# The second layer's output of a token pair by Strassen products of 512-token blocks, in two passes

## The chip, the cores and the metric

One core of a Trainium2 chip runs the whole program. The time is that of the device, in microseconds, from three runs of the kernel before: 595.05 (median), 594.91 and 596.1. A profile of one further execution of the same kernel gives the rows.

## The reference

Retention over q, k, v gives 1536 tokens of 512 features; two gated layers follow, all in float32:

```python
x = attention(q, k, v, lam)            # 1536 x 512
h = np.maximum(x @ moe_w_in, 0)        # 512 -> 2048
x = (h * h) @ moe_w_out                # 2048 -> 512
gate = 1 / (1 + np.exp(-(x @ moe2_w_gate)))   # 512 -> 1536
val = x @ moe2_w_val                   # 512 -> 1536
return (gate * val) @ moe2_w_out       # 1536 -> 512
```

## The kernel before

The tokens form three blocks of 512 (TB). A float32 operand is kept as a high part (a rounded copy, `fp32r`, cast on ScalarE) and a low part (the rest, subtracted on VectorE); a product takes three matmuls: high by high, low by high, high by low. One matmul has 128 x 128 weights and 512 columns of tokens.

Block 0 goes through each layer by itself, unit by unit (a unit is 128 hidden features; 16 in the first layer, 12 in the second): `step_1`, `step_2` (L839, L861). Blocks 1 and 2, the token pair, go through the input side of a layer by Strassen's method: two units and two token blocks make a 2 x 2 problem, seven block products instead of eight, in `strassen` (L646), one call of `block` (L621) for each product, six matmuls in each. The tokens' combinations (T1 to T4) are made by `combine_x` (L554); the weights' (S1 to S4) by `combine_a` (L590), four additions of 128 x 256 on VectorE, after `load_a` (L582) has brought two units from DRAM. `high_a` and `low_a` (L600, L607) split the weights `a` and the sums `as`. In the second layer the keys are (pair i, gate or value), twelve in all; `pair_in_2` (L730) takes the results: gate blocks through the sigmoid, value blocks multiplied by them. The product is a unit's values `g`, 128 features x 512 tokens. `keep_g` (L706) lets the next key store them in DRAM.

After the last key comes the output side of the token pair, `pair_out(2)` (L766): 12 units, each with its values (512 KB) and its output weights (256 KB) loaded by `load_out` and split by `split_out` (L746, L752); per unit 4 column blocks x 2 token blocks x 3 matmuls, into eight banks that stay open from the first to the last unit. At the last unit the banks are copied and stored, the last in two halves on two engines (L798 to L801).

The weights come as float64 and are turned into float32 by `conv_act` and `conv_dve` (two or three operations on ScalarE, three on VectorE) and stored in DRAM as `w32`.

The order of the work is written out by hand. `passed` (L102) counts the matmul time that has been issued (0.2267 us for one, `MM`), and `at(pos, fn)` (L93) puts an operation into its engine's queue when that clock reaches `pos`. T3, T4 and T5 (L881 to L883) are the clock at the start of the second layer's block 0, of the Strassen keys and of the output side. Each engine takes its own queue in order. Tiles come from two pools of 27 buffers (`up`: 128 x 512, `wp`: 128 x 1024), oldest free buffer first; SP issues the loads and stores, and a load waits on SP until its buffer is free. POOL's queue (GpSimd) has no DMAs.

## Time and profile before

| what | us |
|---|---|
| median of the runs | 595.05 |
| the profiled execution | 594.94 |
| its span, first to last instruction | 592.9 |
| TensorE busy | 582.0 |
| VectorE busy | 428.8 |
| ScalarE busy | 349.1 |
| POOL busy | 29.7 |

Engines are PE (TensorE matmul), PEld (its weight load), DVE (VectorE), ACT (ScalarE), POOL (GpSimd) and SP (SyncE, which issues DMAs); a q behind the name is the engine's sequencer. Times are us from the span's start unless marked ns. Matmuls are pipelined: one lasts 389 ns, and the next starts 0.23 us after it.

### The profile page before, as it was taken

The numbers are of one execution on the slowest core, as the hardware profiler recorded it, in microseconds if no ns is written. First come the engines' busy times: TensorE is split into PE (matmuls) and PEld (weight loads), VectorE is DVE, ScalarE is ACT, GpSimd is POOL, SyncE is SP. The second block draws the span as 40 slices with busy tenths as digits, with TensorE's granted clock in tenths as the row PEclk, the third lists the DMA queues.
The fourth block names the chain that finished last, engine by engine and source line by source line (L and its number), as shares of the span: only waits on it lengthen the run. The fifth ranks groups of instructions, "written<-read, shape, count | busy, mean of one in ns | idle before, by whom it ended". The sixth has DMA issues, their size and how long they took to land.

```text
span 592.9 us, 8805 instructions
## 1 busy us (share of the span) xinstructions
PE 582.0 (98%) x3208; PEld 478.7 (81%) x3208; DVE 428.8 (72%) x662; ACT 349.1 (59%) x573; POOL 29.7 (5%) x30
## 2 busy tenths in 40 slices
PE   9899999989999999999999999999999999999997
PEld 8787888767888888888888888888888888888885
DVE  2689896899788868988777787775767786469101
ACT  4679999996655647666457655534455354537101
POOL 1752100000000000000000000000000000000000
PEclk9999999999999999999999999999999999999999
DMA  8999886782163397999968654602233332558003
GB/s 263 413 405 403 286 295 213 256 288 77 71 212 110 111 331 276 414 410 412 405 254 292 250 177 159 179 1 82 96 106 112 137 98 84 193 204 345 0 1 142
DMA packets 52157, 126.94 MB, mean 214 GB/s; under 512 B 5777, under 2 KB 6033, under 8 KB 52114
## 3 DMA queue, kind: packets, MB, share of 16 engines
q1 hardware_dynamic: 51024, 124.15, 58.6%
q10 hardware_dynamic: 1090, 2.24, 1.1%
q8 instruction: 25, 0.41, 0.3%
q14 instruction: 18, 0.15, 0.1%
HBM read 90.71 MB, written 35.66 MB: 213 GB/s over the span
## 4 chain that ended last, share of the span: by engine, by line
PE 88%; DVE 5%; ACT 2%; DMA 2%; issue 2%; POOL 0%; SPq 0%; ACTq 0%; DVEq 0%
PE p L629 32%; PE p L779 26%; PE p L463 15%; PE p L477 10%; PE p L306 2%; PE p L391 2%; DMA decay<-w_dram 1%; DVE at L341 1%; PE p L374 1%; PE p L402 1%; DMA a<-w 1%; DVE m L188 1%; DVE xcl L551 1%; DVE u L180 0%; ACT whi L449 0%
## 5 line engine op out<-in xcount | busy, mean ns | idle before, releaser
L629 PE MATMUL p<-xch,ah 128*128 128x512 f32 x280 | 109.5, 391 | 0.0
L629 PE MATMUL p<-xch,al 128*128 128x512 f32 x280 | 109.0, 389 | 0.0
L629 PE MATMUL p<-xcl,ah 128*128 128x512 f32 x280 | 109.0, 389 | 0.0
L779 PE MATMUL p<-g2h,whi 128*128 128x512 f32 x224 | 87.2, 389 | 0.0
L779 PE MATMUL p<-g2l,whi 128*128 128x512 f32 x224 | 87.1, 389 | 0.0
L779 PE MATMUL p<-g2h,wlo 128*128 128x512 f32 x224 | 87.1, 389 | 0.0
L629 PEld LDWEIGHTS p<-xch,ah 128*128 128x128 f32 x280 | 52.6, 188 | 12.3 <-ACT s L638 1.4
L643 DVE TENSOR_TENSOR c<-p,s 128x512 f32<-128x512 f32 x60 | 41.3, 688 | 28.8 <-PE p L629 22.7
L629 PEld LDWEIGHTS p<-xch,al 128*128 128x128 f32 x280 | 52.6, 188 | 11.1
L629 PEld LDWEIGHTS p<-xcl,ah 128*128 128x128 f32 x280 | 52.6, 188 | 10.6
L638 ACT COPY s<-p 128x512 f32<-128x512 f32 x60 | 35.2, 587 | 37.9 <-PE p L629 37.6
L451 DVE TENSOR_TENSOR wlo<-u,whi 128x512 fp32r<-128x512 f32 x68 | 46.9, 720 | 10.4 <-ACT whi L449 8.4
L155 ACT ACTIVATE j<-raw 128x512 f32<-128x512 f32 x68 | 45.7, 672 | 14.0 <-issue 5.3
L180 DVE CUSTOM_DVE_ANT_0 u<-m,r 128x1024 uint16<-128x1024 uint16 x68 | 48.8, 718 | 5.0 <-ACT r L161 2.0
L779 PEld LDWEIGHTS p<-g2h,whi 128*128 128x128 f32 x224 | 42.1, 188 | 8.8
L779 PEld LDWEIGHTS p<-g2l,whi 128*128 128x128 f32 x224 | 42.1, 188 | 8.7
L779 PEld LDWEIGHTS p<-g2h,wlo 128*128 128x128 f32 x224 | 42.1, 188 | 8.7
L463 PE MATMUL p<-xh,wlo 128*128 128x512 f32 x160 | 43.5, 394 | 3.2 <-DVE wlo L451 3.1
L463 PE MATMUL p<-xh,whi 128*128 128x512 f32 x160 | 43.2, 392 | 0.0
L463 PE MATMUL p<-xl,whi 128*128 128x512 f32 x160 | 42.8, 389 | 0.0
L163 ACT ACTIVATE r<-raw 128x512 int32<-128x512 uint32 x52 | 34.5, 664 | 8.0 <-PE p L779 4.6
L463 PEld LDWEIGHTS p<-xh,wlo 128*128 128x128 f32 x160 | 29.6, 188 | 11.6 <-DVE wlo L451 5.8
(100 smaller groups left out, 922.4 us busy)
## 6 DMA issues: line engine op xcount, KB each, us to landing
raw<-in_w SPq DMA_DIRECT2D x68, 512.0 KB, 6.3
w<-u SPq DMA_DIRECT2D x68, 256.0 KB, 4.7
u<-w SPq DMA_DIRECT2D x64, 256.0 KB, 4.7
g<-g SPq DMA_DIRECT2D x56, 256.0 KB, 4.4
g<-g SPq DMA_DIRECT2D x28, 512.0 KB, 7.5
a<-w SPq DMA_DIRECT2D x20, 512.0 KB, 4.1
kv<-in_kv SPq DMA_DIRECT2D x11, 512.0 KB, 10.3
qk<-in_qk SPq DMA_DIRECT2D x10, 512.0 KB, 9.0
```

The lines of the kernel that those rows point to most:

```text
L155: nc.scalar.activation(j, t[:, :, 1].bitcast(F32), AF.Copy, scale=2.0**-112)
L163: nc.scalar.activation(r, low, AF.Copy, scale=2.0**-29)
L180: nc.vector.tensor_tensor(out=w.bitcast(I32), in0=m, in1=r, op=ALU.add)
L306: nc.tensor.matmul(pv(sc[g])[:, p, :], lhsT=pv(t[:, 1, :])[half(g), p, :], rhs=pv(t[:, 0, :])[half(g), p, :], start=True, stop=True,)
L391: nc.tensor.matmul(o[half(r), p, :], lhsT=v[:, 2 * p + r, :], rhs=pv(at[:, r ^ s, :])[:, p, :], start=p == 0, stop=n == 0 and p == 3, skip ...
L451: lambda lo=lo, src=src, hi=hi: nc.vector.tensor_tensor(out=lo, in0=src, in1=hi, op=ALU.subtract)
L463: nc.tensor.matmul(acc, lhsT=a[:, kk * P : (kk + 1) * P], rhs=b[:, kk, :], start=i == 0, stop=i == 11,)
L477: nc.tensor.matmul(acc[e], lhsT=a[:, e * P : (e + 1) * P], rhs=b, start=first and i == 0, stop=last and i == 2,)
L629: nc.tensor.matmul(acc, lhsT=w[:, col, kk * P : (kk + 1) * P], rhs=x[:, kk, :], start=start and i == 0, stop=stop and i == 5, skip_group_c ...
L638: nc.scalar.copy(s, acc)
L643: nc.vector.tensor_tensor(out=c, in0=acc, in1=s, op=ALU.add)
L779: nc.tensor.matmul(acc[e, t], lhsT=a[:, e * P : (e + 1) * P], rhs=b[:, t, :], start=first and i == 0, stop=last and i == 2,)
```

## The change

The output side of the token pair becomes Strassen products too. The 2 x 2 problem is: two units of a pair by two blocks of 128 output columns, and the two token blocks. There are two passes, one for each half of the 512 output columns. A pass goes through the six pairs; each has seven products of three matmuls of 512 tokens into seven banks, which are combined at the end of the pass. In the second pass pairs 2 and 1 are the last group and go together, and its last product is made in two halves of 256 tokens.

The seven value blocks of a pair are three products of `pair_in_2` as they are and four sums of 512 columns on VectorE (`later`). Pairs 1, 2 and 3 store the seven in DRAM and load them again (`through_dram`; pairs 1 and 2 a second time for the second pass); pairs 0, 4 and 5 are split where they are (`direct`), and the splits of pairs 0, 3, 4 and 5 are kept from the first pass to the second. The seven blocks of the output weights are summed on VectorE in the middle of the second layer (`sum_out_w`) and kept in DRAM; `prepare_w` loads and splits 128 x 896 for each pass and pair.

The sums of the gate and value weights leave VectorE: `load_a` loads the even unit twice into the tile of sums, and `combine_a` issues three DMAs on POOL's queue that add to what is there; the third adds the first's result. The even units' gate and value weights are stored with the other sign; the signs are put right in T1, T2, T4 and in `elem`. `load_a` and `combine_a` of a key stand at the start of the key two before it.

```diff
@@ -171,6 +171,7 @@
+        flip = ph == 2 and u < 2 and f % 2 == 0
...
             lambda: nc.vector.scalar_tensor_tensor(
-                out=m, in0=j, scalar=-(2**31), in1=m, op0=ALU.bitwise_and, op1=ALU.bitwise_or
+                out=m, in0=j, scalar=-(2**31), in1=m, op0=ALU.bitwise_and,
+                op1=ALU.bitwise_xor if flip else ALU.bitwise_or,
...
+        if flip:
+            ops[0] = lambda: nc.vector.tensor_scalar(
+                out=m, in0=j, scalar1=3, scalar2=-(2**31),
+                op0=ALU.logical_shift_left, op1=ALU.bitwise_or,
+            )
...
-            nc.scalar.activation(r, acc[0], AF.Sigmoid)
-            nc.vector.tensor_tensor(out=g, in0=acc[1], in1=r, op=ALU.mult)
+            sign = -1.0 if f % 2 == 0 else 1.0
+            nc.scalar.activation(r, acc[0], AF.Sigmoid, scale=sign)
+            nc.vector.scalar_tensor_tensor(
+                out=g, in0=acc[1], scalar=sign, in1=r, op0=ALU.mult, op1=ALU.mult
+            )
...
+        def minus(name, a, b):
+            t[name] = double("t")
+            nc.vector.scalar_tensor_tensor(
+                out=t[name], in0=t[a], scalar=-1.0, in1=b, op0=ALU.mult, op1=ALU.subtract
+            )
...
+            lambda: diff("T1", b12, b11) if ph == 1 else diff("T1", b11, b12),
...
+            lambda: diff("T2", b22, "T1") if ph == 1 else minus("T2", "T1", b22),
...
+            lambda: diff("T4", b21, "T2") if ph == 1 else minus("T4", "T2", b21),
...
@@ -586,8 +606,28 @@
             out=t.rearrange("p (n h) c -> p n (h c)", n=2),
             in_=w32[ph][2 * i : 2 * i + 2, u].rearrange("n p c -> p n c"),
         )
+        if ph == 2:
+            s = as_t[key] = wp.tile([P, 4, 256], F32, tag="w", name="as")
+            for n in range(2):
+                nc.sync.dma_start(
+                    out=s[:, 2 * n : 2 * n + 2].rearrange("p h c -> p (h c)"),
+                    in_=w32[2][2 * i, u],
+                )
 
     def combine_a(key):
+        ph, i, u = key
+        if ph == 2:
+            s = as_t[key]
+            even, odd = w32[2][2 * i, u], w32[2][2 * i + 1, u]
+            add = dict(accum_op=ALU.add)
+            nc.gpsimd.dma_start(out=s[:, 0:2].rearrange("p h c -> p (h c)"), in_=odd, **add)
+            nc.gpsimd.dma_start(out=s[:, 2], in_=even[:, 256:512], **add)
+            nc.gpsimd.dma_start(
+                out=s[:, 1:4:2], in_=s[:, 0:1].to_broadcast([P, 2, 256]), **add
+            )
+            return
         a = a_t[key]
         s = as_t[key] = wp.tile([P, 4, 256], F32, tag="w", name="as")
...
-        at(pos - 24.0, lambda: load_a(key))
-        at(pos - 15.0, lambda: combine_a(key))
+        at(pos - (24.0 if key[0] == 1 else 42.0), lambda: load_a(key))
+        at(pos - (15.0 if key[0] == 1 else 30.0), lambda: combine_a(key))
...
         part, col = a
+        if key[0] == 2 and part:
+            col = (2, 3, 0, 1)[col]
...
             if n + 2 < len(keys):
                 load_a(keys[n + 2])
+                if key[0] == 2:
+                    combine_a(keys[n + 2])
...
-                combine_a(nxt)
+                if key[0] == 1:
+                    combine_a(nxt)
...
         def use_val(di, t, c, in_psum):
             g = unit("g")
             nc.vector.tensor_tensor(out=g, in0=c, in1=gate.pop((di, t)), op=ALU.mult)
-            keep_g(2, 2 * i + 1 - di, t, g)
+            n = GB.get((di, t))
+            raw[n] = g
+            if n is not None:
+                done(n)
+            if n == 5:
+                later()
+
...
+        def done(n):
+            if i in VIA_DRAM:
+                g = raw[n]
+                at(clock[0] + 2.5, lambda: nc.sync.dma_start(out=gs_dram[i, :, n], in_=g))
+
+        def total(n, a, b, op):
+            raw[n] = unit("gs")
+            nc.vector.tensor_tensor(out=raw[n], in0=raw[a], in1=raw[b], op=op)
+            done(n)
...
+        def later():
+            t = clock[0]
+            at(t + 1.5, lambda: total(0, None, 6, ALU.add))
+            at(t + 3.5, lambda: total(1, 0, 4, ALU.subtract))
+            at(t + 5.5, lambda: total(2, 4, None, ALU.subtract))
+            at(t + 7.5, lambda: total(3, 5, 1, ALU.subtract))
+            at(t + 7.5, lambda: direct(i, raw) if i not in VIA_DRAM else raw.clear())
+    GB = {(0, 0): 4, (1, 0): 5, (1, 1): 6}
+    VIA_DRAM = (1, 2, 3)
+    PIECES = ((0, 1), (2, 3), (4, 5), (6,))
...
+    def new_set(i):
+        both = []
+        for a, b in (("xh", "xr1"), ("xl", "xr2")):
+            if i == 0:
+                s, o = (xp.tile([P, 4, TB], F32R, tag=t, name="gq") for t in (a, b))
+                both.append([s[:, 0:2], s[:, 2:4], o[:, 0:2], o[:, 2:3]])
+            else:
+                p = [double("gq", F32R) for _ in range(3)]
+                both.append(p + [unit("gq1", F32R).rearrange("p (n t) -> p n t", n=1)])
+        gq[i] = both
...
+    def direct(i, raw):
+        pos = clock[0] if i == 0 else DIRECT[i]
...
+        def hi(n):
+            if i not in gq:
+                new_set(i)
+            nc.scalar.copy(block_of(gq[i][0], n), raw[n])
...
+        def lo(n):
+            nc.vector.tensor_tensor(
+                out=block_of(gq[i][1], n), in0=raw.pop(n), in1=block_of(gq[i][0], n),
+                op=ALU.subtract,
+            )
+
+        gap = 2.0 if i == 0 else 0.8
+        for k, n in enumerate((4, 5, 1, 0, 2, 3, 6)):
+            at(pos + gap * k, lambda n=n: hi(n))
+            at(pos + gap * k + 1.2, lambda n=n: lo(n))
...
+    def through_dram(i, load, pos):
...
+        def bring():
+            for p, blocks in enumerate(PIECES):
+                raw[p] = double("gr") if p < 3 else unit("gr1").rearrange("p (n t) -> p n t", n=1)
+            for p in (2, 0, 1, 3):
+                b = PIECES[p]
+                nc.sync.dma_start(out=raw[p], in_=gs_dram[i, :, b[0] : b[-1] + 1])
...
+            nc.scalar.copy(gq[i][0][p], raw[p])
...
+        at(load, bring)
+        for k, p in enumerate((2, 0, 1, 3)):
+            at(pos + 1.1 * k, lambda p=p: hi(p))
+            at(pos + 1.1 * k + 1.3, lambda p=p: lo(p))
+    def sum_out_w(i, pos):
...
+        def load():
+            t["w"] = double("wr")
+            nc.sync.dma_start(
+                out=t["w"], in_=w32[2][2 * i : 2 * i + 2, 2].rearrange("n p c -> p n c")
+            )
...
+        def add():
+            b11, b12, b21, b22 = parts()
+            s = t["s"] = wp.tile([P, 2, 4, P], F32, tag="w", name="ws")
+            for n, a, b in ((0, b12, b11), (1, b22, s[:, :, 0]), (2, b22, b12), (3, b21, s[:, :, 1])):
+                nc.vector.tensor_tensor(out=s[:, :, n], in0=a, in1=b, op=ALU.subtract)
+
+        def store():
+            b11, _, b21, b22 = parts()
+            nc.sync.dma_start(out=wt_dram[i, :, :, 0:4], in_=t.pop("s"))
+            for n, b in ((4, b11), (5, b21), (6, b22)):
+                nc.sync.dma_start(out=wt_dram[i, :, :, n], in_=b)
...
+        at(pos - 9.0, load)
+        at(pos, add)
+        at(pos + 4.0, store)
+    def prepare_w(q, i, load, pos):
...
+        def bring():
+            t["w"] = wp.tile([P, 7, P], F32, tag="w", name="wr")
+            nc.sync.dma_start(out=t["w"], in_=wt_dram[i, :, q])
...
+        def hi():
+            h, _ = wq[q, i] = [wp.tile([P, 7, P], F32R, tag="w", name="wq") for _ in range(2)]
+            nc.scalar.copy(h, t["w"])
...
+        at(load, bring)
+        at(pos, hi)
+        at(pos + 1.2, lo)
+
+
+    PRODUCTS = ((1, 4, 4), (2, 5, 5), (6, 1, 1), (5, 0, 0), (7, 2, 2), (3, 3, 6), (4, 6, 3))
+    STEP = 21 * MM
+    ORDER = (
+        tuple((i,) for i in range(NF2 // 2)),
+        ((5,), (4,), (3,), (0,), (2, 1)),
+    )
+    def blocks_out():
+        for q in range(2):
+            acc, v = {}, {}
...
+            def add(name, k, other, cols=slice(0, TB)):
...
+                nc.vector.tensor_tensor(
+                    out=v[name][:, cols], in0=acc[k][:, cols], in1=v[other][:, cols], op=ALU.add
+                )
...
+            for group in ORDER[q]:
+                first, last = group == ORDER[q][0], group == ORDER[q][-1]
+                for k, gn, wn in PRODUCTS:
+                    if first:
+                        acc[k] = bank()
+                    whole = not (last and q and k == 4)
+                    for cols in (slice(0, TB),) if whole else (slice(0, TB // 2), slice(TB // 2, TB)):
+                        n = 0
+                        for i in group:
+                            (wh, wl), (gh, gl) = wq[q, i], gq[i]
+                            for a, b in ((wh, gh), (wh, gl), (wl, gh)):
+                                nc.tensor.matmul(
+                                    acc[k][:, cols], lhsT=a[:, wn], rhs=block_of(b, gn)[:, cols],
+                                    start=first and n == 0,
+                                    stop=last and n == 3 * len(group) - 1,
+                                    skip_group_check=True,
+                                )
+                                n += 1
+                        if not whole:
+                            add("c21", 4, "u3", cols)
+                            put("c21", 1, 0, cols, nc.sync if cols.start else nc.scalar)
+                    passed(3 * len(group) * MM)
+                    if not last:
+                        continue
+                    if k == 1:
+                        v["s1"] = unit("s1")
+                        nc.scalar.copy(v["s1"], acc[1])
+                    elif k == 2:
+                        add("c11", 2, "s1")
+                        put("c11", 0, 0)
+                    elif k == 6:
+                        add("u2", 6, "s1")
+                    elif k == 5:
+                        add("u4", 5, "u2")
+                    elif k == 7:
+                        add("u3", 7, "u2")
+                        add("c22", 7, "u4")
+                        put("c22", 1, 1, eng=nc.scalar)
+                    elif k == 3:
+                        add("c12", 3, "u4")
+                        put("c12", 0, 1)
+                    elif whole:
+                        add("c21", 4, "u3")
+                        put("c21", 1, 0)
...
@@ -960,7 +1214,7 @@
+        for i in range(NF2 // 2):
+            sum_out_w(i, T3 + 14.0 + 10.0 * i)
...
-        at(T4 - 20.0, lambda: load_a((2, 0, 1)))
-        combine_x([T4 - 46.0 + 3.5 * k for k in range(11)])
+        at(T4 - 32.0, lambda: load_a((2, 0, 1)))
+        at(T4 - 20.0, lambda: combine_a((2, 0, 1)))
+        combine_x(2, [T4 - 46.0 + 3.5 * k for k in range(11)])
...
-        for f in range(NF2):
-            prepare_out(2, f, T5 + 24 * MM * f)
+        for k in range(1, 6):
+            if k in VIA_DRAM:
+                through_dram(k, T5 - 12.0 + 4.0 * k, T5 - 11.0 + 5.2 * k)
+            else:
+                DIRECT[k] = T5 - 11.0 + 5.2 * k
+        for k in range(6):
+            prepare_w(0, k, T5 - 14.0 + STEP * k, T5 - 7.0 + STEP * k)
+        T6 = T5 + 6 * STEP
+        for k, i in enumerate((5, 4, 3, 0, 2, 1)):
+            prepare_w(1, i, T6 - 9.0 + STEP * k, T6 - 3.5 + STEP * k - (2.5 if k == 5 else 0))
+        through_dram(2, T6 + 1.0, T6 + 7.0)
+        through_dram(1, T6 + 6.0, T6 + 12.0)
-        pair_out(2)
+        blocks_out()
```

## Rows read from the trace of the kernel before

**Rows 1.** The page's first part: span; busy us, share and instructions of each engine.
```profile
span 592.9 us, 8805 instructions
PE 582.0 (98%) x3208; PEld 478.7 (81%) x3208; DVE 428.8 (72%) x662; ACT 349.1 (59%) x573; POOL 29.7 (5%) x30
```

**Rows 2.** The chain of waits in order of time: start, length, engine and line, instructions.
```profile
19.60 1.09 PE p L306 x16
...
139.39 2.09 PE p L463 x8
...
523.38 65.31 PE p L779 x288
588.71 0.38 ACT o L800
...
589.11 0.42 DVE o L800
```

**Rows 3.** Busy time by stretches, columns in the first line.
```profile
core 0: us, PE busy (x) PEld busy (x) DVE busy (x) ACT busy (x) POOL busy (x), PEclk, DMA share, GB/s
220.00:310.00 90.00, 90.00 (x398) 74.49 (x397) 76.38 (x115) 56.64 (x87) 0.00 (x0) 1.00 0.93 361
320.00:380.00 60.00, 60.00 (x266) 49.69 (x265) 47.19 (x73) 34.41 (x59) 0.00 (x0) 1.00 0.61 200
444.20:463.20 19.00, 19.00 (x85) 15.73 (x85) 13.61 (x23) 9.27 (x14) 0.00 (x0) 1.00 0.35 111
533.00:543.00 10.00, 10.00 (x46) 8.29 (x45) 9.07 (x10) 7.78 (x11) 0.00 (x0) 1.00 1.04 406
```

**Rows 4.** VectorE's timeline: start, length, instruction, idle before it and its releaser.
```profile
461.97 0.69 DVE L643 TENSOR_TENSOR c<-p,s 128x512 f32<-128x512 f32 x1 [1.36 <-PE p L629]
...
468.89 1.22 DVE L610 TENSOR_TENSOR al<-as,ah 128x1024 fp32r<-128x1024 f32 x1
...
517.49 0.69 DVE L759 TENSOR_TENSOR wlo<-u,whi 128x512 fp32r<-128x512 f32 x1 [4.58 <-ACT whi L755]
...
519.58 0.68 DVE L643 TENSOR_TENSOR c<-p,s 128x512 f32<-128x512 f32 x1
...
523.56 0.68 DVE L759 TENSOR_TENSOR wlo<-u,whi 128x512 fp32r<-128x512 f32 x1
524.16 1.22 DVE L760 TENSOR_TENSOR g2l<-g,g2h 128x1024 fp32r<-128x1024 f32 x1
525.30 0.68 DVE L739 TENSOR_TENSOR g<-p,r 128x512 f32<-128x512 f32 x1
...
584.63 0.69 DVE L792 COPY o<-p 128x512 f32<-128x512 f32 x1 [33.41 <-PE p L779]
```

**Rows 5.** The same of SP's and ScalarE's queues around key 6's cast of sums.
```profile
448.10 0.37 SPq L585 DMA_DIRECT2D a<-w  x1
...
467.59 1.06 ACT L604 CAST ah<-as 128x1024 fp32r<-128x1024 f32 x1 [1.03 <-DVE as L598]
468.70 0.59 ACT L638 COPY s<-p 128x512 f32<-128x512 f32 x1
```

**Rows 6.** DMA: packets and issues (KB, us to landing), 525 to 545; then 406, 586, whole.
```profile
DMA packets 2568, 6.91 MB, mean 346 GB/s; under 512 B 287, under 2 KB 287, under 8 KB 2568
g<-g SPq DMA_DIRECT2D x9, 512.0 KB, 7.8
...
g<-g SPq DMA_DIRECT2D x23, 256.0 KB, 4.3
...
out_t<-o SPq DMA_DIRECT2D x3, 256.0 KB, 2.1
...
kv<-in_kv SPq DMA_DIRECT2D x11, 512.0 KB, 10.3
```

**Rows 7.** VectorE's groups by line and form: busy us, mean ns, idle before.
```profile
L451 DVE TENSOR_TENSOR wlo<-u,whi 128x512 fp32r<-128x512 f32 x33 | 21.0, 686 | 7.3 <-ACT whi L449 5.4 <-DMA u<-w 0.8 <-issue 0.7
...
L188 DVE SCALAR_TENSOR_TENSOR m<-j,m 128x512 int32<-128x512 int32 x11 | 7.6, 693 | 0.4
...
L185 DVE TENSOR_SCALAR m<-j 128x512 int32<-128x512 int32 x11 | 4.6, 420 | 0.0
...
L596 DVE TENSOR_TENSOR as<-a 128x256 f32<-128x256 f32 x11 | 4.6, 418 | 0.0
```

More of the change, by code (lines that the diff above doesn't have):

```diff
@@ L192, in conv_dve @@
         ]
+        if flip:
[3 more added lines that the diff above has]
+            )
         if sign:
+            assert not flip
             ops.pop(1)
@@ L552, in split_x, with combine_x @@
         )
-    def combine_x(places):
+    def combine_x(ph, places):
         x1, x2 = xr[1], xr[2]
@@ new lines, in block_of @@
+    def block_of(pieces, n):
+        return pieces[n // 2][:, n % 2]
+    def direct(i, raw):
+        pos = clock[0] if i == 0 else DIRECT[i]
+        raw = dict(raw)
+        def hi(n):
[11 more added lines that the diff above has]
+            at(pos + gap * k + 1.2, lambda n=n: lo(n))
@@ new lines, in retention_moe_kernel, with hi, lo @@
+    DIRECT = {}
+    def through_dram(i, load, pos):
+        raw = {}
+        def bring():
[4 more added lines that the diff above has]
+                nc.sync.dma_start(out=raw[p], in_=gs_dram[i, :, b[0] : b[-1] + 1])
+        def hi(p):
+            if i not in gq:
+                new_set(i)
+            nc.scalar.copy(gq[i][0][p], raw[p])
+        def lo(p):
+            nc.vector.tensor_tensor(
+                out=gq[i][1][p], in0=raw.pop(p), in1=gq[i][0][p], op=ALU.subtract
+            )
[3 more added lines that the diff above has]
+            at(pos + 1.1 * k + 1.3, lambda p=p: lo(p))
@@ new lines, in prepare_w, with lo @@
+    def prepare_w(q, i, load, pos):
+        t = {}
+        def bring():
[4 more added lines that the diff above has]
+            nc.scalar.copy(h, t["w"])
+        def lo():
+            h, l = wq[q, i]
+            nc.vector.tensor_tensor(out=l, in0=t.pop("w"), in1=h, op=ALU.subtract)
+        at(load, bring)
+        at(pos, hi)
+        at(pos + 1.2, lo)
@@ new lines, in retention_moe_kernel, with put @@
+    PRODUCTS = ((1, 4, 4), (2, 5, 5), (6, 1, 1), (5, 0, 0), (7, 2, 2), (3, 3, 6), (4, 6, 3))
[7 more added lines that the diff above has]
+            acc, v = {}, {}
+            def put(name, t, e, cols=slice(0, TB), eng=nc.sync):
+                col = (t + 1) * TB
+                eng.dma_start(
+                    out=out[2 * q + e, :, col + cols.start : col + cols.stop],
+                    in_=v[name][:, cols],
+                )
+            def add(name, k, other, cols=slice(0, TB)):
+                if name not in v:
+                    v[name] = unit(name)
+                nc.vector.tensor_tensor(
+                    out=v[name][:, cols], in0=acc[k][:, cols], in1=v[other][:, cols], op=ALU.add
+                )
+            for group in ORDER[q]:
[14 more added lines that the diff above has]
+                                    skip_group_check=True,
+                                )
+                                n += 1
[25 more added lines that the diff above has]
+                        put("c21", 1, 0)
+                for i in group:
+                    wq.pop((q, i))
+                    if q or i < 3 and i:
+                        gq.pop(i)
@@ L785, in pair_out @@
                     copy = nc.scalar.copy if t == 0 else nc.vector.tensor_copy
-                    if ph == 1:
-                        copy(xr[t + 1][:, e, :], acc[e, t])
-                        continue
-                    dst = out[e, :, (t + 1) * TB : (t + 2) * TB]
-                    if (e, t) != (3, 1):
-                        o = unit("o")
-                        copy(o, acc[e, t])
-                        (nc.scalar if t == 0 and e < 3 else nc.sync).dma_start(out=dst, in_=o)
-                        continue
-                    for c, copy, eng in (
-                        (0, nc.scalar.copy, nc.scalar),
-                        (TB // 2, nc.vector.tensor_copy, nc.sync),
-                    ):
-                        o = unit("o")[:, 0 : TB // 2]
-                        copy(o, acc[e, t][:, c : c + TB // 2])
-                        eng.dma_start(out=dst[:, c : c + TB // 2], in_=o)
+                    copy(xr[t + 1][:, e, :], acc[e, t])
     prev = []
```

21 lines of the change are left out of this document (13 added, 8 removed).

## The prediction

> **What bounds the kernel now.** I read the page's busy shares first: TensorE is busy 98% of the span, VectorE 72%, ScalarE 59% [rows 1]. A busy TensorE need not be at its pace, so the chain of waits came next. From 139.39 us to 588.71 us it is 32 pieces, all TensorE; what waits there are lies in the attention part ahead of them, and the output stage that the change replaces is one unbroken piece of 288 matmuls in 65.31 us, 0.2268 us each [rows 2]. So before 588.71 us a matmul less is 0.2268 us less, as long as operands, banks and queues keep up. The table by stretches shows what is in reserve: the granted clock is 1.00 and TensorE full in each; VectorE is busy 13.6 of 19 us while one pair of units is made, 9.1 of 10 us just after the output stage begins [rows 3], and has nothing to do for the 33.4 us before its next to last copies [rows 4]. Behind the last matmul come a half copy on ScalarE, one on VectorE that waited for it, and a store, till 592.9 [rows 1, 2].
>
> I write S for 523.4 us, where the output stage begins; on the code's own clock it is T5. A key is one of the twelve Strassen products before S: 42 matmuls, 9.52 us; key 6 begins near 464.7.
>
> **The change part by part.**
>
> *Matmuls.* 12 units x 24 = 288 become 2 column halves x 6 pairs x 7 products x 3 = 252. 36 x 0.2268 = 8.2 us less. The last six matmuls are each cut into two of 256 columns. No row has that form. Below, half of 0.2268 each costs nothing; above, a full 0.2268 each costs 6 x 0.2268 = 1.4 us. Sixteen matmuls of 128 columns take 1.09 us, 0.068 each [rows 2], so the weight load does not hold a short matmul at the long one's pace: I take 0.1 us.
>
> *The tail.* Before: ScalarE's half copy, 0.38, then VectorE's, 0.42, then the store [rows 2]. Now VectorE's addition of the last half reads the bank with no copy of ScalarE's ahead: 0.4 us less.
>
> *VectorE in the first half of the new stage.* This is where the gain can go. Seven blocks of values are split for a pair where four were, twice for pairs 1 and 2, and twelve times 896 columns of weights where 512 were. From the starts of VectorE's own instructions when they queue: 0.60 us for 512 columns (523.56 to 524.16), 1.14 for 1024 (524.16 to 525.30) [rows 4]; 896 lie between, 1.0. The first low half of pair 1 can start near S-4.9: ScalarE's cast for it stands behind the copy of S1 x T1 in the last key, which TensorE ends at S-6.8; copy 0.59 and cast 1.06 [rows 5] follow. Up to the low half of weights 3, VectorE then has in order: pairs 1 and 2, 3 x 1.14 + 0.6 each, 8.0; three of four pieces of pair 3, 3.4; weights 1, 2 and 3, 3.0; the last key's seven additions and products at 0.6, 4.2, which before too began at S-3.8 [rows 4]; the four sums of the last pair, 2.4. Together 21.0: it ends at S+16.1. TensorE wants it after three pairs of 21 matmuls, at S+14.3: a wait of 1.8, with semaphores 2.0. The same sum for weights 2 (14.2 us, done at S+9.3, wanted at S+9.5) and for the first value of the last pair (S+22.5, wanted at S+23.8) gives none. Bounds: 0 if casts come earlier than their places; with unqueued durations, 0.69 and 1.22, the list is 23.7 long and the wait 4.5; with loads 1.5 us late besides, 6. I take 2.0. In the second half the list is some 17 us in 28.6: nothing.
>
> *Loads of that stage.* Before, 512 KB landed in 7.8 us while the engines moved 346 GB/s, since all came after S [rows 6]. The new ones start as buffers of the last keys come free, from about S-18: 5.5 MB of values for pairs 1 to 3 and 2.8 MB of weights by S+14, 8.3 MB in 32 us, 260 GB/s: nothing on the path, and if they lag, it is in the 6 above.
>
> *Sums of the gate and value weights by DMA.* VectorE loses 8 additions a pair at 0.42 [rows 7] and gains 4 sums of 512 columns at 0.69: 2.8 for 3.4, and pair 0's seven splits, 4.8 us over two keys, fit the 5.4 of 19 that are idle [rows 3]. The added wait is ScalarE's: its cast of the sums waits for three DMAs on POOL's queue, the third of which waits for the other two. Behind the cast stands ScalarE's copy of S1 x T1, and for that TensorE's fourth block of the key: in key 6 the copy ends at 469.29 [rows 5], the block begins at 464.7 + 5.44 = 470.1, 0.8 us of slack. The time there is: the load that feeds the cast at 467.59 was issued at 448.10 [rows 5], since SP runs ahead until a buffer of an older key is free. The two new loads are issued about 1 us behind it. With 4.3 us to land [rows 6] and X for each of two adding DMAs in a row, the sums are ready 1 + 4.3 + 2X after 448.10, and must be by 20.3 (19.5 and the slack): X up to 7.5. Keys 7, 9 and 11 have less: ahead of their load stand now, in SP's order, stores of split values up to the pair's second sum, which VectorE reaches some 7 us into the key; the load moves from 2.5 to 7.2 us into it, and X may be 5.2. No row has an adding DMA, nor any on POOL's queue. Bounds for 256 KB: 2.1 (an output store) and 10.3 (the slowest row, of 512 KB, as if what is read and added counted double) [rows 6]. I take 4.3, the row of the same size in the same stage: no wait, 1.8 us to spare in the tight keys.
>
> The Trainium skill's "DMA: Bandwidth & Descriptors", section "Anatomy of one DMA — SWDGE (gpsimd) path", gives 2.0 us plus bytes over 436 GB/s for a DMA of POOL's queue, an estimate of 2.6 us for 256 KB, with nothing said of adding; by it the sum stays and the spare time is 5.2 us. The nearest row says 4.3.
>
> *Sums of the output weights, between 325 and 385 us.* 24 additions of 256 columns at 0.42 [rows 7], 10 us, on a VectorE that is busy 47.2 of 60 us there [rows 3]. What is left, 2.7 us, is their cover; without it the splits of the next unit come late. Their 8.3 MB in 60 us come to 200 GB/s that move there now; the stage before moved 361 [rows 3]. Between 0 and 2 us; I take 0.2.
>
> *The signs.* Second operations in instructions that are there already: a three-operand form takes 693 ns where the plain split takes 686 [rows 7]. Nothing; if the shift went from 420 ns to 690, 12 x 0.27 = 3.2 us, spread over conversions that are not due.
>
> *Sum.* 594.94 (the profiled execution: span 592.9 and 2.0 around it) - 8.2 + 0.1 - 0.4 + 2.0 + 0.2 = 588.6; the median of the runs shown, 595.05, is 0.1 higher: 588.8 rounded up.
>
> **The rivals.**
> *1. VectorE's list decides the stage.* For: 21 us in a row, where 9.1 of 10 were full before [rows 3]. Against: before, it stood idle 4.6 us just ahead [rows 4]. With the long durations and pair 1 late by 2 us and more, and a wait between 325 and 385 us, 5 to 8 us are lost: 592 to 595.5, most of the gain.
> *2. The adding DMAs take too long (the slower side).* Place: ScalarE's cast of the sums, keys 2 to 11. It costs from X = 5.2 and decides from 6.5: three tight keys x 2 x 1.3 = 7.8, 596.5. For: three DMAs in a row, each reading what it writes. Against: nothing else is on POOL's queue. At X = 8.3 all keys are 1.6 late over two keys, 0.8 a key for nine, 7, and the tight ones 4 more each: 588.8 + 19 = 608; at 10.3 it is 2.7 a key and 4 more thrice: 625.
> *3. POOL's issue waits for VectorE.* VectorE runs 8.1 us of a key without a gap, thirteen instructions from 461.97 on [rows 4]. An issue held till such a run ends waits 8.1 x 8.1 / (2 x 9.52) = 3.4 us on average; two in the chain make X 7.7 in effect: 0.1 a key and 5 in each tight one, 16 us: 605. Against: in that stage VectorE's rows are TENSOR_TENSOR at 0.69 for 512 columns, none at the shift's 0.42 [rows 4, 7]. The Trainium skill's "SBUF — State Buffer", section "Who interferes with whom", says that VectorE's two-port forms, copies and one-operand arithmetic, keep POOL from the memory altogether, and that two-operand additions do not take the port that writes; by that rule the rows speak against this rival.
> *4. All is hidden:* 594.94 - 8.2 + 0.1 - 0.4 = 586.4, if the casts run 2 us ahead of where I put them.
>
> **How the numbers follow.** Forecast 588.8, chance 0.60, its own range 587.2 to 592. Rival 1: 0.17 (0.10 faster, 0.07 no change). Rival 2: 0.13 (slower). Rival 3: 0.04 (0.03 slower, 0.01 no change). Rival 4: 0.06. Within 0.2%, 1.2 us, can't be told from no change here. So faster 0.60 + 0.10 + 0.06 = 0.76, the same 0.08, slower 0.16. The range goes from 586.3 (rival 4 within) to 598 (rival 1 and the mild end of rival 2 within); about 0.13 is left out above.
>
> **What would show it.** Right: 252 matmuls' worth in the last stage, S to its end about 59 us; one TensorE wait near S+14 for a low half on a VectorE that is unbroken from S-5 to S+27; ScalarE's cast of the sums some 3 us into the key as before; adding DMAs near 4.3 us. Wrong: waits of TensorE inside the keys for ScalarE's copy behind a cast that waits for POOL's DMA; waits between 325 and 385 us; 5 us or more of waits after S; or waits for a bank where the column halves meet.

## The result and the profile after

The changed kernel takes 597.94 us (median of 10 runs, 596.57 to 601.98), the kernel before 594.9 in the same comparison: a ratio of 1.0058, with an interval of 1.0038 to 1.0078. It is slower, by 0.6%; 588.8 us was forecast. Its runs spread with TensorE's granted clock: the four with a mean of 0.998 or more take 596.6 to 597.5 us, the six below it 597.5 to 602.0. The profiled execution, one of the six, took 598.35 us; its span is 3.7 longer than before. The page's first part, as [rows 1]:

```profile
span 596.6 us, 9061 instructions
PE 578.2 (97%) x3178; PEld 472.4 (79%) x3178; DVE 464.2 (78%) x702; ACT 366.9 (62%) x599; POOL 65.6 (11%) x66
```

TensorE is busy 3.8 us less, in a longer span. What it waited for (total us, times, longest), without the rows of the attention part and of the units' weights:

```profile
PE p L671 <- ACT s L680: 4.7, 3, 2.1
...
PE p L975 <- DVE wq L930: 1.3, 2, 0.8
...
PE p L671 <- DVE c L685: 0.6, 1, 0.6
...
PE p L975 <- DVE c L960: 0.5, 1, 0.5
```

L671 is the matmul of the Strassen keys, L975 that of the new output stage. The first row is the sign that the prediction had named for its slower rival: TensorE waits inside the keys for ScalarE's copy. The chain of waits (start, length, what), as [rows 2]:

```profile
310.77 10.88 PE p L471 x48
...
457.20 6.59 DMA as<-w
464.31 0.86 POOL as L626
465.16 3.80 issue
468.98 3.81 DMA as<-as
...
473.89 0.59 ACT s L680
474.52 4.54 PE p L671 x12
...
497.44 26.25 PE p L671 x114
...
532.72 8.88 PE p L975 x39
...
592.32 0.99 PE p L975 x6
```

Before, this chain is TensorE alone from 139.39 us on [rows 2]. Now a load, two adding DMAs and a copy (457.20 to 474.48) are a part of it. Its pieces say where the time went; the kernels of the last four columns are told below:

| us in the profiled execution | before | after | value stores later | sums on VectorE | adding DMAs alone | sums on VectorE, weight sums later |
|---|---|---|---|---|---|---|
| up to T3 | 310.9 | 310.8 | 311.4 | 310.7 | 311.1 | 311.3 |
| block 0, T3 to T4 | 95.2 | 96.8 | 96.8 | 96.8 | 95.2 | 96.7 |
| keys, T4 to S | 117.3 | 125.2 | 121.4 | 120.2 | 118.3 | 120.2 |
| output stage | 65.3 | 60.6 | 60.5 | 60.2 | 65.3 | 60.1 |
| behind the last matmul | 4.2 | 3.3 | 3.3 | 3.2 | 4.1 | 3.2 |
| span | 592.9 | 596.6 | 593.3 | 591.1 | 594.0 | 591.4 |

The output stage gave 4.7 us and the tail 0.9. The keys took 7.9, block 0 another 1.6. The queues around the longest wait, as [rows 5]: SP's, POOL's, ScalarE's and TensorE's timelines (start, length, instruction, idle before it and its releaser):

```profile
453.46 2.66 SPq L797 DMA_DIRECT2D gs<-gs  x2
456.22 0.39 SPq L605 DMA_DIRECT2D a<-w  x1
456.69 0.93 SPq L612 DMA_DIRECT2D as<-w  x2
...
462.22 0.91 POOL L625 DMA_DIRECT2D as<-w  x1 [9.08 <-ACT ah L644]
464.31 0.86 POOL L626 DMA_DIRECT2D as<-w  x1 [1.17 <-DMA as<-w]
468.98 1.21 POOL L627 DMA_DIRECT2D as<-as  x1 [3.82 <-DMA as<-w]
...
472.94 1.04 ACT L644 CAST ah<-as 128x1024 fp32r<-128x1024 f32 x1 [3.97 <-DMA as<-as]
473.89 1.07 ACT L680 COPY s<-p 128x512 f32<-128x512 f32 x2
...
474.52 0.50 PE L671 MATMUL p<-xch,ah 128*128 128x512 f32 x1 [2.09 <-ACT s L680]
474.86 0.40 PE L671 MATMUL p<-xcl,ah 128*128 128x512 f32 x1
```

Read downwards: stores of values, of which three more stand before these two, hold SP's queue from 448.15 on, and the three loads come behind them; the first adding DMA goes out 6.0 us after the first load, the second 2.1 us later, since it waits for the other load; the one that adds the first's result goes out at 468.98 and lands 3.8 us later; ScalarE, idle for 3.97 us, runs the cast and then the copy that TensorE waits for. The same idle time on the same releaser comes twice more, 3.86 us before 495.86 and 1.66 before 515.00: the casts for keys 7, 9 and 11 and no others.

Busy time by stretches, as [rows 3]; the third stretch is the twelve matmuls after that wait:

```profile
core 0: us, PE busy (x) PEld busy (x) DVE busy (x) ACT busy (x) POOL busy (x), PEclk, DMA share, GB/s
320.00:380.00 60.00, 59.04 (x260) 48.19 (x259) 50.24 (x88) 30.13 (x52) 2.90 (x3) 1.00 0.99 330
444.20:463.20 19.00, 19.00 (x86) 15.61 (x85) 16.49 (x24) 11.12 (x19) 3.92 (x4) 1.00 0.86 235
474.50:479.10 4.60, 4.58 (x13) 3.61 (x14) 2.04 (x4) 1.09 (x2) 1.21 (x1) 0.63 0.92 209
```

The DMA engines, 0.35 busy over a pair of keys before, are 0.86 busy, and 0.99 instead of 0.61 at 320 to 380. The granted clock, 1.00 in every stretch of [rows 3], is 0.63 behind the wait of 2.09 us: most of the twelve matmuls start 0.43 us apart instead of 0.23, which is the lower of the clock's two levels (1.2 GHz). They take 4.54 us where twelve take 2.72.

DMA issues of the keys (KB each, median us to landing), as [rows 6]:

```profile
as<-w SPq DMA_DIRECT2D x18, 256.0 KB, 5.7
...
as<-w POOLq DMA_DIRECT2D x9, 256.0 KB, 4.5
as<-as POOLq DMA_DIRECT2D x9, 256.0 KB, 4.9
...
as<-w POOLq DMA_DIRECT2D x9, 128.0 KB, 5.6
```

VectorE's timeline, as [rows 4], at one place of block 0 and one of the output stage:

```profile
339.33 0.42 DVE L904 TENSOR_TENSOR ws<-wr,ws 128x256 f32<-128x256 f32 x1
...
341.46 1.88 DVE L459 TENSOR_TENSOR wlo<-u,whi 128x512 fp32r<-128x512 f32 x3
...
547.15 1.08 DVE L930 TENSOR_TENSOR wq<-wr,wq 128x896 fp32r<-128x896 f32 x1
```

From 338.20 to 341.46 four output-weight sums (the last is copied) and a conversion's three operations stand ahead of the low half `wlo` of a unit's weights; TensorE waits 0.60 us for it at 342.20, and 0.36 in the same way at 351.02. At 547.15 VectorE reaches the low half of weights 3 after a list without a gap; it ends at S+15.5, and TensorE has waited 0.81 us.

### The profile page after: what moved, and what is told of

Read it like the earlier page. It is cut to its first block, busy times and chain, and to the rows that moved or that the text cites. A ratio compares the mean times of both kernels' runs of the same rounds, so it can differ in the third digit from the quotient of the medians.

```text
span 596.6 us, 9061 instructions
## 1 busy us (share of the span) xinstructions
PE 578.2 (97%) x3178; PEld 472.4 (79%) x3178; DVE 464.2 (78%) x702; ACT 366.9 (62%) x599; POOL 65.6 (11%) x66
## 4 chain that ended last, share of the span: by engine, by line
PE 74%; DVE 9%; DMA 7%; issue 5%; ACT 5%; POOL 1%; ACTq 0%; SPq 0%; DVEq 0%; POOLq 0%
PE p L671 24%; PE p L1048 15%; PE p L471 14%; PE p L485 9%; PE p L975 7%; PE p L314 2%; PE p L399 2%; DMA as<-as 1%; DMA wr<-wt 1%; DMA decay<-w_dram 1%; DMA as<-w 1%; DVE at L349 1%; DVE m L189 1%; PE p L382 1%; PE p L410 1%
## 5 line engine op out<-in xcount | busy, mean ns | idle before, releaser
L671 PE MATMUL p<-xch,ah 128*128 128x512 f32 x280 | 110.5, 394 | 5.3 <-ACT s L680 4.7
L671 PE MATMUL p<-xch,al 128*128 128x512 f32 x280 | 109.7, 392 | 0.0
L671 PE MATMUL p<-xcl,ah 128*128 128x512 f32 x280 | 109.6, 392 | 0.0
L671 PEld LDWEIGHTS p<-xch,ah 128*128 128x128 f32 x280 | 53.0, 189 | 19.3 <-ACT s L680 7.3
L671 PEld LDWEIGHTS p<-xch,al 128*128 128x128 f32 x280 | 52.9, 189 | 11.1
L671 PEld LDWEIGHTS p<-xcl,ah 128*128 128x128 f32 x280 | 53.0, 189 | 10.8
L975 PE MATMUL p<-gq,wq 128*128 128x512 f32 (+1 forms) x258 | 58.9, 387 | 1.8 <-DVE wq L930 1.3
L975 PEld LDWEIGHTS p<-gq,wq 128*128 128x128 f32 x258 | 47.4, 188 | 13.4 <-DVE wq L930 3.0
L625 POOL DMA_DIRECT2D as<-w x12 | 12.1, 1007 | 347.1 <-PE p L471 287.8
L1048 PE MATMUL p<-g2l,whi 128*128 128x512 f32 x128 | 49.8, 389 | 0.0
L1048 PE MATMUL p<-g2h,wlo 128*128 128x512 f32 x128 | 49.8, 389 | 0.0
L1048 PE MATMUL p<-g2h,whi 128*128 128x512 f32 x128 | 49.8, 389 | 0.0
L457 ACT CAST whi<-u 128x512 fp32r<-128x512 f32 x68 | 38.0, 614 | 1.5 <-PE p L485 1.0
```

The costliest lines, as they stand in the source:

```text
L457: nc.scalar.copy(hi, src)
L625: nc.gpsimd.dma_start(out=s[:, 0:2].rearrange("p h c -> p (h c)"), in_=odd, **add)
L671: nc.tensor.matmul(acc, lhsT=w[:, col, kk * P : (kk + 1) * P], rhs=x[:, kk, :], start=start and i == 0, stop=stop and i == 5, skip_group_c ...
L975: nc.tensor.matmul(acc[k][:, cols], lhsT=a[:, wn], rhs=block_of(b, gn)[:, cols], start=first and n == 0, stop=last and n == 3 * len(group) ...
L1048: nc.tensor.matmul(acc[e, t], lhsT=a[:, e * P : (e + 1) * P], rhs=b[:, t, :], start=first and i == 0, stop=last and i == 2,)
```

## The experiments

### The adding DMAs, the output side, or both

Four kernels make a square. In one the output side stays as changed and the sums are VectorE's again:

```diff
-            nc.gpsimd.dma_start(out=s[:, 0:2].rearrange("p h c -> p (h c)"), in_=odd, **add)
...
+            tt(out=s[:, 0], in0=a11, in1=a21, op=ALU.add)
+            tt(out=s[:, 2], in0=a21, in1=a22, op=ALU.add)
+            tt(out=s[:, 3], in0=a22, in1=s[:, 0], op=ALU.add)
+            tt(out=s[:, 1], in0=a12, in1=s[:, 3], op=ALU.add)
```

> The changed kernel with the sums of the gate and value weights as four additions of 256 columns on VectorE again, no adding DMA and no second load of the even unit. Theory A and theory B both expect the waits for the cast of sums to go: the keys take 117.3 to 119 us, 591 to 593 us in all. A third theory C (VectorE is the bound of the keys once it has the value sums too, and the DMAs only took the place of that) expects TensorE to wait for VectorE or for copies behind it by 4 us or more in the keys: 596 or more.

593.47 us, ratio 0.9973 [0.9961, 0.9985]: faster than before, 0.5 above the range that A and B expect, and far from C. The waits behind the adding DMAs are gone, but the keys still take 120.2 us: TensorE waits 0.62 and 0.96 us for ScalarE's copy among the casts of pair 0 (443.48 and 454.25; ahead of the second, ScalarE stands 1.73 us for VectorE's key sums) and 0.60 at the end.

The other has the adding DMAs and the signs with the output side of before, and what prepares it:

```diff
-        blocks_out()
+        pair_out(2)
```

> The kernel before with the signs, the double load and the adding DMAs alone; the output side, its stores and its splits as before. Theory A: with the stores of values held to the next key as before, the load of a key keeps about two keys' time, the cast of sums waits nowhere, and the time is that of before within 0.5 us (594.5 to 595.5). Theory B: TensorE waits in most keys, 598 or more.

595.82 us, ratio 1.0012 [1.0001, 1.0023]: 0.3 above theory A's range, far from B's. In its keys TensorE waited once:

```profile
PE p L670 <- ACT s L679: 0.8, 1, 0.8
```

and in this stretch the DMA share is no lower than in the changed kernel:

```profile
440.00:460.00 20.00, 20.00 (x90) 16.56 (x89) 11.32 (x15) 10.07 (x16) 6.01 (x6) 1.00 0.94 231
```

| median us | sums on VectorE | adding DMAs |
|---|---|---|
| output side as before | 595.0 | 595.8 |
| Strassen output side | 593.5 | 597.9 |

The adding DMAs alone cost 0.8 us (0.1 to 1.4 by the interval), the output side alone gains 1.5. Independent, both together would give 594.3; the 3.6 us above that, some 1.5 either way by the three intervals together, come of their meeting. With the adding DMAs alone a key's loads go out on SP every 9.5 us (the next at 459.08 and 468.60), and the chain of DMAs fits:

```profile
440.04 0.37 SPq L604 DMA_DIRECT2D a<-w  x1
...
449.56 0.37 SPq L604 DMA_DIRECT2D a<-w  x1
```

In the changed kernel they go out at 440.24, 456.22, 460.19 and 476.29: every second one is late. The DMAs themselves are no faster alone; the issues of its keys (406 to 524), where the changed kernel has 5.7 and 4.9 us:

```profile
as<-w SPq DMA_DIRECT2D x18, 256.0 KB, 5.4
...
as<-as POOLq DMA_DIRECT2D x9, 256.0 KB, 6.3
```

### SP's order

```diff
-                at(clock[0] + 2.5, lambda: nc.sync.dma_start(out=gs_dram[i, :, n], in_=g))
+                at(clock[0] + 12.0, lambda: nc.sync.dma_start(out=gs_dram[i, :, n], in_=g))
```

> The changed kernel with the stores of the split pairs' values put 12.0 us on the clock behind the value instead of 2.5, so that in SP's order the next key's load stands ahead of them; nothing else. Theory A (those stores hold the loads of keys 7, 9 and 11 back, and the three adding DMAs then miss the cast): the three waits of TensorE in the Strassen keys (2.1, 2.0 and 0.2 us) and the slow clock after the first (1.8 us) go, the keys take 118.5 us instead of 124.9, about 592 us in all. Theory B (the adding DMAs are too slow by themselves under this load, whenever they begin): waits of 1 to 2 us stay in at least two keys, 596 us or more.

593.87 us, ratio 0.9974 [0.996, 0.9988], nearer to theory A. The stores now stand behind the next loads, and 3.8 of the 7.9 us in the keys are back. TensorE's waits at the two places:

```profile
474.39 0.50 PE L671 MATMUL p<-xch,ah 128*128 128x512 f32 x1 [1.38 <-ACT s L680]
484.76 0.50 PE L671 MATMUL p<-xch,ah 128*128 128x512 f32 x1 [0.53 <-ACT s L680]
```

2.09 and 1.98 us became 1.38 and 0.53, and the clock is 1.00 in the stretches behind both. So the order of SP's queue makes half of the keys' loss. Not all: the load of key 7's sums goes out at 453.50, 3.8 us earlier in its key (this run's keys begin 0.6 us later), but its cast starts at 472.81, only 0.7 us earlier, because the last adding DMA, issued at 465.21, needs 7.4 us; the stores run beside the adding DMAs now, with a DMA share of 1.05 to 1.15 from 474 to 489. How much of the rest is this traffic, and how much POOL's own order (a key's last DMA ahead of the next key's first), no run parts.

The three loads on ScalarE's queue were the second try:

```diff
-        nc.sync.dma_start(
+        (nc.scalar if ph == 2 else nc.sync).dma_start(
...
-                nc.sync.dma_start(
+                nc.scalar.dma_start(
```

> The changed kernel with the second layer's three loads of a key (both rows, and the first row twice) issued by ScalarE instead of SyncE; adding DMAs, stores and everything else unchanged. Theory A, it is SyncE's order (value stores ahead of the loads) that makes keys 7, 9 and 11 late: their loads go out at the key's start, the waits of 4.7 us and the slow clock after the longest go, 592.5 to 594 us. Theory B, the chain of load, adding DMA, adding DMA is long by itself with 16 DMA engines 0.85 to 0.95 busy: more than half of the waits stays, 595.5 us or more.

608.78 us, ratio 1.0227 [1.0198, 1.0255]. By the number it is theory B, but the run doesn't test it: ScalarE reaches the loads in its own order, at 418.20, 424.20, 438.57, 444.65 and 460.01, every second one late again, and eight waits of 11.3 us in all follow.

### Block 0: the output-weight sums

```diff
-                nc.vector.tensor_tensor(out=s[:, :, n], in0=a, in1=b, op=ALU.subtract)
+                nc.gpsimd.tensor_tensor(out=s[:, :, n], in0=a, in1=b, op=ALU.subtract)
```

> The changed kernel with the 24 subtractions for the output weights issued on POOL instead of VectorE. If VectorE's list is what makes TensorE wait between 340 and 351 us, the 1.6 us that block 0 of the second layer takes longer than before go (95.2 us from 310.8 on instead of 96.8), 596 us in all. If the added DMA traffic is (the engines' share is 0.98 at 320 to 340 us), the 1.6 us stay.

600.21 us, ratio 1.0087 [1.0059, 1.0115], not the 596 expected; block 0 takes 97.0 us. The waits for `wlo` are gone, two for ScalarE's `gh` (0.28 and 0.64 us) came. While GpSimd subtracts (343.2 to 346.9) VectorE's operations of 0.69 us take 1.1:

```profile
343.32 1.14 DVE L189 SCALAR_TENSOR_TENSOR m<-j,m 128x512 int32<-128x512 int32 x1
344.50 1.11 DVE L181 CUSTOM_DVE_ANT_0 u<-m,r 128x1024 uint16<-128x1024 uint16 x1
```

The next run moves the sums behind the conversions:

```diff
-            sum_out_w(i, T3 + 14.0 + 10.0 * i)
+            sum_out_w(i, T3 + 48.0 + 8.0 * i)
```

> The changed kernel, with the six output-weight sums (loads, four subtractions each, stores) moved from 325 to 375 us to 359 to 399 us (one every 8 us), behind the last conversions of weights. Theory A, the four subtractions ahead of a low half of weights on a VectorE that is 90% busy at 340 to 360 cost block 0 its 1.6 us: the waits at 342.20 and 351.02 go, the block takes 95.2 to 95.5 us instead of 96.8, about 596.3 us. Theory B, the traffic does it (DMA share 0.9 to 1.0 at 340 to 360, 0.6 before): with the loads and stores at 350 to 404 beside the keys' own first loads, as much is lost there, 597.5 us or more.

605.04 us, ratio 1.0173 [1.0133, 1.0213]; neither theory had this. The waits at 342.20 and 351.02 are gone, as theory A says, but one of 1.55 us for a cast came at 401.19, and the last sums' stores are now ahead of key 2's load on SP (411.35; 387.31 in the changed kernel):

```profile
409.15 2.15 SPq L910 DMA_DIRECT2D wt<-wr  x3
411.35 0.61 SPq L605 DMA_DIRECT2D a<-w  x1
```

```profile
431.44 0.80 PE L671 MATMUL p<-xch,ah 128*128 128x512 f32 x1 [5.49 <-ACT s L680]
```

Behind these 5.49 us the granted clock is 0.56 from 431.4 to 436. It is a late load and the adding chain once more, by another store.

### The rest of the loss, without adding DMAs

First the low halves of the output weights on GpSimd, in the changed kernel:

```diff
-            nc.vector.tensor_tensor(out=l, in0=t.pop("w"), in1=h, op=ALU.subtract)
+            nc.gpsimd.tensor_tensor(out=l, in0=t.pop("w"), in1=h, op=ALU.subtract)
```

> The changed kernel, with the low halves of the output weights (12 subtractions of 128x896, the tile whose lateness held TensorE 0.81 us at 548.28 and 0.46 us at 582.77) computed by GpSimd instead of VectorE. Theory A, VectorE's unbroken list from 528 to 564 is what makes these halves late: both waits go, the output stage shortens by 1.3 us or a little more, about 596.5 us against 597.9 of the changed kernel. Theory B, GpSimd is the worse place: its subtractions of 128x256 took 0.73 to 1.19 us where the weight sums were put on it, which is 2.6 to 4.1 us for 128x896, and VectorE's copies of 0.69 us took 1.1 us beside them; then the waits stay or change their name, 598 us or more. Keys and block 0 stay as in the changed kernel in both.

603.87 us, ratio 1.017 [1.0119, 1.0222]: theory B. The output stage takes 65.6 us, all that it had gained. VectorE's third sum of values is 0.68 us in the changed kernel (540.33); here it and the operation behind it take 2.61 us each while GpSimd's two run:

```profile
541.01 2.61 DVE L801 TENSOR_TENSOR gs<-gs,g 128x512 f32<-128x512 f32 x1
543.54 2.61 DVE L876 TENSOR_TENSOR gq<-gr,gq 128x512 fp32r<-128x512 f32 x1
...
540.16 5.44 POOL L930 TENSOR_TENSOR wq<-wr,wq 128x896 fp32r<-128x896 f32 x2 [4.84 <-ACT gq L873]
```

Additions with one operand in a PSUM bank (`c<-p,s`) stay at 0.68. The Trainium skill's "SBUF — State Buffer", section "Who interferes with whom", says that a VectorE instruction with two inputs in SBUF contends with a GpSimd instruction that reads SBUF, and that one with at most one such input, outside its two-port modes, does not. The trace agrees, 2.61 against 0.68 us.

Then all three: sums on VectorE, weight sums later (48 + 8i), low halves on GpSimd; and the same with `gap` 3.4 for pair 0 instead of 2.0:

> The three repairs together: the keys' sums on VectorE again with no adding DMA, the output-weight sums behind the conversions, and the low halves of the output weights on GpSimd. If each is worth what its own run says: 593.5 of the first alone, less 1.6 (weight sums later), less 1.3 (low halves): 590.6 us, and 592 if GpSimd's subtraction gives nothing. Rival: with 24 subtractions more at 359 to 399 and the keys' four additions, VectorE is over 85% busy from 360 to 520 and gives a part back as waits in the keys: 592.5 us or more.

> As the three repairs together, and the seven casts of pair 0's blocks 3.4 us apart instead of 2.0. In the kernel with the sums on VectorE, TensorE waited for ScalarE's copy 0.62 us at 443.48 and 0.96 us at 454.25, both among these casts. Theory A, the casts' crowding makes these waits: they go, 1.0 to 1.6 us below the run of the three repairs (about 589.3 us). Theory B, they only move along with the casts, or the four-block additions on VectorE make them: within 0.4 us of that run.

598.34 us, ratio 1.0051 [1.0034, 1.0068], and 600.27, 1.0079 [1.0053, 1.0104]. The first is far above its 590.6: an output stage of 65.8 us, spoilt in the same way, not the waits in the keys that its rival expected. Block 0 takes 95.8 us, so the place of the sums was worth 1.0 there. In the second the waits of 0.62 and 0.92 us among pair 0's casts (442.73, 453.48) became 1.15 and 0.79 at 461.03 and 463.47: by the traces, which both span 596.4 us, they move along, theory B. Its median is 1.9 us above the first's all the same: its four runs have a mean granted clock of 0.996 or 0.997, the first's 0.999 or 1.00.

With the low halves on VectorE, and the weight sums at 46 + 7i:

```diff
-            sum_out_w(i, T3 + 14.0 + 10.0 * i)
+            sum_out_w(i, T3 + 46.0 + 7.0 * i)
```

> The keys' sums on VectorE again (no adding DMA, no second load), and the six output-weight sums from T3+46 on, one every 7 us, behind the conversions; the low halves stay on VectorE. Theory A, the two losses are independent: 593.5 us of the sums on VectorE alone, less the 1.0 us that block 0 came out shorter with the sums later (95.8 us from T3 to T4 against 96.8): 592.5 us, with the output stage as in that run (0.83 us at its first wait for a low half). Theory B, the later sums push VectorE's preparation of the keys back: 593.5 us or more, with new waits between 390 and 460.

593.45 us, ratio 0.997 [0.9959, 0.9981], where 593.47 had been measured without the move: theory B. The two waits in block 0 went and one of their size came, for a cast:

```profile
396.64 1.22 DVE L582 SCALAR_TENSOR_TENSOR t<-t,xr 128x1024 f32<-128x1024 f32 x1
...
397.89 1.05 ACT L560 CAST xch<-t 128x1024 fp32r<-128x1024 f32 x1 [3.76 <-DVE t L582]
...
399.51 1.20 PE L471 MATMUL p<-xh,whi 128*128 128x512 f32 x4 [0.97 <-ACT whi L457]
```

The cast `whi` stands on ScalarE behind the cast of a token combination (`t`), which VectorE ends only at 397.86: four weight sums (388.78 to 390.3) and four key sums (395.17 to 396.7) are in its list ahead. The same loss, at another crowded place.

```diff
-            prepare_w(0, k, T5 - 14.0 + STEP * k, T5 - 7.0 + STEP * k)
+            prepare_w(0, k, T5 - 18.0 + STEP * k, T5 - 11.0 + STEP * k)
...
-            prepare_w(1, i, T6 - 9.0 + STEP * k, T6 - 3.5 + STEP * k - (2.5 if k == 5 else 0))
+            prepare_w(1, i, T6 - 14.0 + STEP * k, T6 - 5.0 + STEP * k - (2.5 if k == 5 else 0))
```

> As the run with both repairs, and the output weights prepared earlier: the first six loads, casts and low halves 4 us earlier, the loads of the last six 5 us earlier and their casts 1.5 us. Theory A, the waits for low halves near 15.7 us and 49.8 us into the output stage come from VectorE's unbroken list (first) and from a load that lands after 8.7 us (second): both go, 1.3 us below the run with both repairs, or a little more. Theory B, VectorE has no room before the output stage either (9.4 of 10 us busy at 520 to 530): the earlier low halves delay the last copies of the keys, the wait at the stage's start (0.60 us) grows, and less than 0.4 us is won.

593.42 us, ratio 0.9976 [0.9966, 0.9987]: no gain, theory B. The first wait for a low half (0.81) went, the one at the stage's start grew from 0.60 to 0.88 us and the second from 0.32 to 1.37.

```diff
-                eng.dma_start(
+                (eng if q else nc.scalar).dma_start(
...
-            sum_out_w(i, T3 + 46.0 + 7.0 * i)
+            sum_out_w(i, T3 + 46.0 + 6.0 * i)
```

> As the run with the output weights earlier, with two more edits: the first half's four output stores all issued by ScalarE (SyncE stood 4.1 us at three of them, 555.5 to 559.6, with the loads of the second half's weights and values behind it), and the weight sums every 6 us instead of every 7, so that the last one ends ahead of VectorE's work at 394 to 399. Theory A, SyncE's order makes the second half's loads late, and with them the wait of 1.37 us at 578.49: that wait goes, and with it most of the 0.97 us at 398.9: about 591.2 us, against 593.4. Theory B, the wait at 578 is VectorE's own list (eight low halves of values between 566 and 577, the weights' low halves behind them): it stays, 592.5 us or more.

595.67 us, ratio 1.0014 [0.9999, 1.003], over a wide spread (593.24 to 599.28) that goes with the granted clock: 1.00 in the runs up to 594.34 us, 0.997 or less from 595.45 on; what lowered it isn't shown, since the profiled execution has 1.00. The wait at 578 became 0.38 and 1.12: theory B. The one at 399 stayed at 0.97, with the last weight sums gone from behind the token combination and four others still ahead of it (388.64).

So three kernels without adding DMAs are below both, at 593.4 to 593.5 us, 1.5 us of the 8.2 that the matmuls are worth; the one that keeps the adding DMAs and stores the values later is at 593.87.

## Why the prediction was wrong

The step that failed is "I take 4.3 ...: no wait, 1.8 us to spare in the tight keys", and with it the odds of rival 2.

*The adding DMAs.* Place and keys are the rival's; its mechanism, slow adding DMAs, is only a part. Their landing times were near in the median, 4.5 and 4.9 us for 4.3. (The Trainium skill's "DMA: Bandwidth & Descriptors", section "Anatomy of one DMA — SWDGE (gpsimd) path", gave an estimate of 2.6 for a plain one; the adding ones of this trace took longer, and these decide.) In the two keys that made TensorE wait they were 6.5 and 3.8 (key 7), 6.6 and 4.9 (key 9). From the first load to the sums I had 1 + 4.3 + 2 x 4.3 = 13.9 us; key 7's chain takes 472.9 - 456.22 = 16.7. The loads land in 5.7, with the DMA engines 0.86 busy; the second adding DMA went out 2.1 us behind the first, for its own load, and the third waits for both, 6.8 us behind the first where I had 4.3; an issue on POOL takes 0.9 to 1.2 us, and I had none. That is 2.8 us over, on 1.8 to spare. The load was late too: it went out 8.4 us into key 4, which begins at 447.8, for the 7.2 I had, because VectorE ends the pair's second sum only at 455.8. With these 1.2 us the sum gives a wait of 2.2, and TensorE waited 2.09. Key 9's chain, 476.29 to 495.7, is longer still, 19.4 us.

With the adding DMAs alone the DMAs are as slow and TensorE hardly waits, and with the stores later half of the loss is gone: that the late load is the main cause is shown. How the rest divides stays open.

Nor is a wait its own length only. It ends a pipeline: the matmul ahead runs out (0.39 us instead of 0.23) and the second one behind starts 0.34 us after the first, 0.27 in all. And behind the 2.09 us the slow clock cost 1.55 more in the profiled execution. Two waits (4.07 together), two restarts (0.54) and the clock make 6.2 of the keys' 7.9 us.

*The rest of the keys.* I let pair 0's splits fit into VectorE's idle time. They do; but its seven casts among ScalarE's copies made a wait of 0.61 us, and low halves of loaded values ahead of the last key's additions on VectorE one of 0.60: 1.7 us with restarts.

*Sums of the output weights:* 1.6 us for 0.2, inside the bounds of 0 to 2. Over 60 us VectorE had room; ahead of the low halves at 341.46 and 350.29, where conversions still run, it had not: its list has no gap from 336.31 and from 346.42 on.

*The output stage.* The wait for the low half of weights 3 is where it was put (S+14.3; TensorE stopped at S+14.7), its list ends at S+15.5 for 16.1, and it costs 0.81 us and a restart for 2.0. Two that I had at nothing came: 0.46 us at 582.77 for another low half, and 0.52 at 592.32, where the last product's second half waits until VectorE has read the first from the same bank. Waits and restarts make 2.6 us; the half matmuls start 0.14 us apart, 0.3 more than six full ones. 252 x 0.2268 + 2.6 + 0.3 = 60.1; measured 60.6, and the 0.5 I can't place. 4.7 us gained where 6.1 were forecast: the mechanism was right.

*The tail* gave 0.9 for 0.4. The copy that went is worth the 0.4; behind the last operation on VectorE the span ends 2.9 us later where it was 3.4, which I had at nothing. *The signs* cost nothing that shows: up to T3 the kernels are equal, and with the signs but no output-weight sums block 0 takes 95.2 us as before. *Rival 3* falls: no issue on POOL takes longer than 1.75 us.

By terms: 588.6 forecast, with 7.9 (keys), 1.4 (block 0), 1.4 (output stage) and -0.5 (tail) makes 598.8, for 598.35 of the profiled execution.

## What to carry to other kernels

Add up a chain of DMAs that feed each other with its issues, its loads and the traffic that it makes itself, and hold it against the least spare time of any iteration. Where a store of late data shares a queue with a load for a later iteration, the store sets when the load goes out. Room in an engine's mean is not room in the stretch where the work falls: three moves of the same work only moved the wait.

## What was not expected of the hardware

The length of a wait does not tell whether the clock falls behind it. It fell to its lower level behind waits of 2.09 us (0.63 granted over 4.6 us), 4.12 (0.50; key loads on ScalarE), 5.49 (0.56; weight sums later) and, with pair 0's casts spread, behind two of 0.99 and 0.78 that end 1.7 us apart. It stayed at 1.00 behind 1.98, 2.13 (key loads on ScalarE) and 3.33 us (weight sums on POOL). What decides, no run shows. One case of either kind, stretches in the columns of [rows 3]; first pair 0's casts spread, then the weight sums on POOL:

```profile
544.20:547.00 2.80, 2.74 (x6) 1.82 (x6) 2.80 (x2) 0.19 (x1) 1.96 (x1) 0.51 0.00 0
```

```profile
476.30 0.50 PE L671 MATMUL p<-xch,ah 128*128 128x512 f32 x1 [3.33 <-ACT s L680]
...
476.30:480.90 4.60, 4.60 (x20) 3.83 (x21) 3.56 (x6) 1.70 (x3) 1.21 (x1) 1.00 0.70 162
```

Two-operand operations of VectorE in SBUF stood while GpSimd subtracted, 2.61 us for 0.68.
